# A fused attention and gated-MLP kernel on one core: where the normalization of v runs, and in which order its weights arrive

## The chip, the cores and the metric

The kernel runs on one core of a Trainium2 chip. The metric is the time of one execution on the device in microseconds (us). Five executions were timed. One execution was recorded by the hardware profiler; every duration below comes from that record. The engines are named as the profile does: PE is TensorE's matmul (PEld its loading of weights), DVE is VectorE, ACT is ScalarE, POOL is GpSimd, and SP is SyncE, which here only issues DMAs. POOL issues DMAs too, between its own computations and in the same order of instructions.

## The reference

Batch 8, 8 heads, sequence 576, head dimension 64. Linear attention with a learned feature map, then a gated MLP with a spatial (over the sequence) matrix:

```python
def phi(x):
    proj = np.einsum('bhsd,df->bhsf', x, w_phi)                  # d_feat 128
    proj = proj - np.max(np.abs(proj), axis=-1, keepdims=True)
    return np.concatenate([np.exp(proj), np.exp(-proj)], axis=-1)
q_p, k_p = (phi(q), phi(k))
kv = np.einsum('bhsf,bhsd->bhfd', k_p, v)
z = np.sum(k_p, axis=2)
num = np.einsum('bhsf,bhfd->bhsd', q_p, kv)
den = np.einsum('bhsf,bhf->bhs', q_p, z)[..., None] + 1e-06
x = num / den                                                    # heads side by side: 576 x 512
h = np.maximum(x @ w_in, 0.0)                                    # 576 x 1024
u, v = h[..., :d_ff // 2], h[..., d_ff // 2:]
v_n = (v - mean(v)) / np.sqrt(var(v) + 1e-06)                    # over the 512 columns
v_s = np.einsum('ts,bsd->btd', w_spatial, v_n) + b_spatial[None, :, None]
out = (u * v_s) @ w_out                                          # 576 x 512
```

## The kernel before

The sequence of a batch is cut into four blocks of 128 positions and a tail of 64. Work on q, k and the attention goes by units: a unit is two heads of one batch (the main blocks), four units to a batch, and one more unit holds the tails of two batches. Units are numbered in order: 0 and 1 are batch 0, 2 is the tails of batches 0 and 1, 3 and 4 batch 0 again, 5 to 8 batch 1, 9 the tails of batches 2 and 3, 10 to 13 batch 2, and so on.

step(i) (line 636) writes the instructions of one step of a software pipeline. At step i different stages of several units meet: keys (projection by TensorE, maxima mk by VectorE at line 279, features kf by ScalarE, and a_scale at line 299: em by ScalarE, then vs, v times em, by GpSimd at line 307, vst for tails at line 322), queries (maxima mq, and their split into two bf16 halves, mhl, at lines 296 and 297, which GpSimd does from unit 5 on), maxima (a transpose of mhl, line 328), query features, the products kv and num, and xT.

After each stage, fill (line 620) takes tasks of the MLP from a queue by a credit of TensorE time. b_tasks (line 592) makes the tasks of one batch: v (b_v and b_v_tail: matmul, relu by ScalarE, mean and variance by VectorE), the root 1/sqrt(var + 1e-6) on GpSimd (root, line 454: add, pow, product with the mean, change of sign), the normalization of v by one multiply-add per block (line 465, on GpSimd; vn for the four blocks, vnt for the tail), u (b_u), the spatial matmuls (b_s, lines 524 and 525: four blocks of vn and the tail) with their product by u on VectorE (line 527), and the output matmuls of the batch before. Batch 0 also transposes the spatial matrix there (transpose_spatial) and copies the spatial bias, four copies by ScalarE, into the row of w_spT that a row of ones in vnt picks up.

From batch 2 on (XB) k and q are transposed by DMAs that SP issues (cross, line 116), three steps ahead, and the query maxima are merged into the query projection through the wide weights wm. These hold, per head, w_phi and a row that subtracts the maximum; weights_with_max writes them on GpSimd at steps 6 and 7, twelve small instructions. A copy of half of q's transpose (q_even, tile qt) goes by another DMA on SP, one step ahead of the unit.

Loads are given to steps by at(step, ...), and stand after the step's other instructions: k, q and the weights on POOL's queue (with a cast from fp32 to bf16), v on SP's. What goes through pin stays in the order in which it was written on its engine; the other instructions are put in order by a scheduler. In the profile all that goes through pin has the line 61, so it is told apart by its tile.

Of the kernel before, what the change touches and what calls it, by code (L numbers as in the profile page):

```python
# [8 lines left out]
FP32 = mybir.dt.float32  # L9
# [7 lines left out]
def kernel(  # L17
# [116 lines left out]
    for n, t in enumerate((k, q)):  # L134
        for i in range(2):
            pin(nc.sync.dma_start)(out=tails[i * TL:(i + 1) * TL, n * H:(n + 1) * H, :], in_=tail_ap(t, i))
    load_v(0, 0)
# [43 lines left out]
    for i in range(2):  # L181
        fill_vnt(i, nc.gpsimd.tensor_copy)
    for x in ("k", "q"):
        pin(nc.gpsimd.tensor_copy)(out=half_tile(x, 0, 0)[:, 2:4], in_=first[x, 2])
# [9 lines left out]
    wsp = s2.tile([P, NB, T0], BF16, tag="vn", name="wsp", bufs=2)  # L194
    wspr = cpool.tile([P, NB, TL], BF16)
    wspt = s2.tile([TL, S], BF16, tag="ob", name="wspt", bufs=6)
    bsp_row = s2.tile([P, S], FP32, tag="xT", name="bsp_row", bufs=3)
    nc.sync.dma_start(out=bsp_row[TL:TL + 1, :], in_=moe_b_spatial)
    nc.sync.dma_start(out=bsp_row[0:1, :], in_=moe_b_spatial)
# [10 lines left out]
    def transpose_spatial(i):  # L210

        pt = psum.tile([P, S], BF16, tag="bank", name="pt")
        if i < NB:
            sc = POS[i]
            for tp, c in enumerate(POS):
                nc.tensor.transpose(out=pt[:, tp * P:(tp + 1) * P], in_=wsp[:, c, bass.ds(sc, P, step=NB)],
                                    identity=ident)
            nc.tensor.transpose(out=pt[:, T0:S], in_=wspt[:, bass.ds(sc, P, step=NB)],
                                identity=ident[:TL, :TL])
            nc.vector.tensor_copy(out=w_spT[:, i, :], in_=pt)  # L220
            return
        for bl in range(2):
            lo = bl * TL
            for tp, c in enumerate(POS):
                nc.tensor.transpose(out=pt[lo:lo + TL, tp * P:(tp + 1) * P], in_=wspr[:, c, :], identity=ident)
            nc.tensor.transpose(out=pt[lo:lo + TL, T0:S], in_=wspt[:, T0:S], identity=ident[:TL, :TL])
            nc.vector.tensor_copy(out=w_spT[lo:lo + TL, NB + bl, :], in_=pt[lo:lo + TL, :])
        for bl, row in ((0, TL), (1, 0)):
            r = slice(row, row + 1)
            pin(nc.scalar.copy)(  # L230
                out=w_spT[r, NB + bl, 0:T0].rearrange("o (a b p) -> o a b p", a=2, b=2),
                in_=bsp_row[r, 0:T0].rearrange("o (p b a) -> o a b p", a=2, b=2))
            pin(nc.scalar.copy)(out=w_spT[r, NB + bl, T0:S], in_=bsp_row[r, T0:S])


    def merged(u):
        return u["pair"] and u["b"] >= XB

    def weights_with_max(n):
        for j in range(4 * n, 4 * n + 4, 2):  # L240
            pin(nc.gpsimd.tensor_copy)(out=wm[:, j, :], in_=wphi2[:, 0:F])
            pin(nc.gpsimd.tensor_tensor)(out=wm[:, j + 1, :], in0=wphi2[:, F:2 * F], in1=sel[:, j + 1, :], op=ALU.add)
            pin(nc.gpsimd.tensor_copy)(out=wm[D:D + 2 * H, j, :], in_=sel[0:2 * H, j, :])
# [40 lines left out]
    def a_queries(u):  # L284

        m, early = mhl[u["i"] % NM], u["i"] < EARLY
        if not early:
            mq = small.tile([P, H], FP32, tag="mq", name="mq")
        for half in range(2):
            pq = by_token(u["qT"], half)  # L290
            if early and half == 0:
                mq = pq[:, 0, 0:H]
            nc.vector.tensor_reduce(out=mq[:, 4 * half:4 * half + 4], in_=pq, axis=AX.X, op=ALU.max,  # L293
                                    apply_absolute_value=True)
        eng = nc.vector if early else nc.gpsimd
        eng.tensor_copy(out=m[:, 0:H], in_=mq)
        eng.tensor_tensor(out=m[:, H:2 * H], in0=mq, in1=m[:, 0:H], op=ALU.subtract)

    def a_scale(u):
# [3 lines left out]
        if u["pair"]:  # L303
            pj = u["pj"]
            vs = feat.tile([P, 2, H, DA], BF16, tag="vs", name="vs", bufs=4)
            for s in range(2):
                nc.gpsimd.tensor_tensor(out=vs[:, s, :, 0:D], in0=st[u["b"]]["v"][:, pj * H:(pj + 1) * H, :],  # L307
                                        in1=em[:, s, :].unsqueeze(2).to_broadcast([P, H, D]), op=ALU.mult)
            nc.gpsimd.tensor_copy(out=vs[:, :, :, D:DA], in_=em.unsqueeze(3).to_broadcast([P, 2, H, 2]))
# [144 lines left out]
    def root(mv, r, n):  # L454

        var = small.tile([P, NB, 1], FP32, tag="var", name="var")
        rs = small.tile([P, NB, 2], FP32, tag="rs", name="rs")
        nc.gpsimd.tensor_scalar(out=var[r, 0:n], in0=mv[r, 0:n, 1:2], scalar1=1e-6, scalar2=None, op0=ALU.add)
        nc.gpsimd.tensor_tensor(out=rs[r, 0:n, 0:1], in0=var[r, 0:n], in1=neghalf[r, 0:n].unsqueeze(2), op=ALU.pow)
        nc.gpsimd.tensor_tensor(out=var[r, 0:n], in0=mv[r, 0:n, 0:1], in1=rs[r, 0:n, 0:1], op=ALU.mult)  # L460
        nc.gpsimd.tensor_scalar(out=rs[r, 0:n, 1:2], in0=var[r, 0:n], scalar1=-1.0, scalar2=None, op0=ALU.mult)
        return rs

    def normalize(dst, src, rs):
        nc.gpsimd.tensor_scalar(out=dst, in0=src, scalar1=rs[:, 0:1], scalar2=rs[:, 1:2],  # L465
                                op0=ALU.mult, op1=ALU.add)

    def b_v(b, j):
# [7 lines left out]
        v_mm(lambda kc: d["xT"][:, kc, j * P:(j + 1) * P], d["vr"][j], slice(0, P), stats, d["mv"][:, j, :])  # L476

    def b_root(b):
        st[b]["rs"] = root(st[b]["mv"], slice(0, P), NB)

    def b_ln(b, j):
        d = st[b]
        normalize(d["vn"][:, j, :], d["vr"][j], d["rs"][:, j, :])

    def b_v_tail(g, bls):
# [6 lines left out]
        rstd = root(mv, r, 1)  # L492
        for bl in bls:
            r = slice(bl * TL, (bl + 1) * TL)
            normalize(vnt[g % 2][r, bl, :], vr[r], rstd[r, 0, :])
# [96 lines left out]
    def b_tasks(b):  # L592
# [8 lines left out]
        ts.append((0.0, lambda: b_root(b)))  # L601
        if b == 0:
            ts += [(0.3, lambda i=i: transpose_spatial(i)) for i in range(NB + 1)]
        for y in range(NB):
            ts += ns[y:y + 1] + outs[2 + y:3 + y] + us[y:y + 1]
# [75 lines left out]
    at(1, load_v, 1)  # L681
    at(2, load, "k", 1, 0)
# [4 lines left out]
    at(4, load_weight, wspt, moe_w_spatial[T0:S, :])  # L687
    at(5, tail_scale, 0, 1)
    at(5, load_weight, wsp, rows[:, :, 0:T0])
    at(5, load_weight, wspr, rows[:, :, T0:S])  # L690
    at(6, load_weight, w_in_bf[:, :, 0:HALF], cols[:, :, 0:HALF])
    at(8, load_weight, w_out_bf, moe_w_out.rearrange("(kc p) f -> p kc f", p=P))
    for u in units:
        i = u["i"]
        if not u["pair"] and u["g"] > 0:
            early = 1 if u["g"] > 1 else 0
            at(i - AT - early, load_tail, "k", u["g"])
            for x in ("q", "v"):
                at(i - AT + 1 - early, load_tail, x, u["g"])
        if u["pair"] and u["b"] >= XB:  # L700
            if u["pj"] == 0:
                for n, (x, y) in enumerate((("k", 0), ("q", 0), ("k", 1), ("q", 1))):
                    at((4, 4, 6, 7)[n] if u["b"] == XB else i - AB + n, load, x, u["b"], y)
# [4 lines left out]
    at(6, weights_with_max, 0)  # L708
    at(7, weights_with_max, 1)
# [39 lines left out]
```

## Time and profile before

| | |
|---|---|
| median of 5 runs | 285.83 us (284.72 to 286.02) |
| the profiled execution | 285.86 us, of it span 283.77 us |
| mean granted clock of TensorE | 0.987 of full |
| busy: PE, DVE, ACT, POOL | 260.4, 231.4, 219.4, 200.6 us |
| vn and vnt on POOL, line 465 | 40 instructions, 0.77 us each |
| vs on POOL, line 307 | 64 instructions, 1.04 us each |
| pow of the root on POOL, line 459 | 8 of 1.05 us (128x4) and 8 of 0.58 us (64x1) |
| the other three instructions of a root on POOL | 0.19 to 0.25 us each |
| the wm writes on POOL | 12 instructions, 0.28 to 0.43 us each |
| one load issued on POOL | 0.56 to 0.82 us |
| the four bias copies on ACT | 1.11 us (two of 1x512), 0.24 us (two of 1x64) |
| DMA engines, mean busy share | 7 to 9 tenths in each slice up to 205 us |

The span is the time from the first to the last recorded instruction. Busy time is the union of an engine's instructions. Matmuls are pipelined, so PE counts as busy also where it only waits for a matmul to drain; the distance between the starts of two matmuls says more. In the chain of waits each piece is the work that the next one waited for, or its neighbour on the same engine, followed back from the end. A line of a timeline gives start, duration, engine, line of the kernel, operation, output and input tiles and their shapes, and in brackets how long the engine stood idle before it and what released it.

### The profile page before, as it was taken

The page shows a single profiled execution, that of the slowest core. Times are in us where ns is not written, and L with a number is a line of the kernel's source. Part 1 is how long each engine was busy: PE and PEld are TensorE (multiplying, and loading weights), DVE is VectorE, ACT ScalarE, POOL GpSimd, SP SyncE. Part 2 cuts the span into 40 slices and gives each one's busy share as a digit, 9 for nine tenths or more (in the row PEclk, how much of TensorE's full clock was granted, in tenths as well). Part 3 has the DMA queues.
Part 4 walks back from the last instruction along what each step waited for, and adds up shares of the span by engine and source line. Part 5 has one row for each costly group of instructions (what it writes and reads, how often), then busy time and mean ns, then how long its engine had stood idle before and what let it go on. Part 6 is the DMA issues. An engine that isn't in the chain of part 4 may idle for free.

```text
span 283.8 us, 8175 instructions
## 1 busy us (share of the span) xinstructions
PE 260.4 (92%) x3042; PEld 173.2 (61%) x3042; DVE 231.4 (82%) x576; ACT 219.4 (77%) x499; POOL 200.6 (71%) x362
## 2 busy tenths in 40 slices
PE   2768987987999999999999999999999999999993
PEld 1457875764666576666666675666666765654441
DVE  7969996875699988998889989997889897566441
ACT  5669996979299997899889987899789977723601
POOL 5897999999958895799949984889548832411710
PEclk9979999999799999999999999999999999999999
DMA  8998999999977999979989999999765301120305
GB/s 195 218 229 102 157 140 242 142 145 215 173 96 154 131 239 195 161 217 208 191 110 130 205 192 162 233 204 225 101 121 132 86 2 58 55 76 37 112 3 185
DMA packets 85148, 42.43 MB, mean 150 GB/s; under 512 B 52146, under 2 KB 80498, under 8 KB 85108
## 3 DMA queue, kind: packets, MB, share of 16 engines
q1 hardware_dynamic: 60020, 30.95, 54.0%
q0 software_dynamic: 24928, 10.89, 36.9%
q8 instruction: 24, 0.39, 0.6%
q14 instruction: 16, 0.13, 0.2%
q10 hardware_dynamic: 160, 0.07, 0.1%
HBM read 32.85 MB, written 9.44 MB: 149 GB/s over the span
## 4 chain that ended last, share of the span: by engine, by line
PE 61%; POOL 16%; ACT 7%; DVE 6%; DMA 5%; issue 3%; SPq 0%; POOLq 0%; ACTq 0%; DVEq 0%
PE ps L524 10%; PE po L549 9%; PE pv L448 9%; PE ps L267 6%; PE pu L503 6%; ACT kf L282 4%; PE pv L379 4%; PE pn L399 4%; PE pq L345 3%; POOL vs L307 3%; DMA q_bf<-in_q_dram 3%; PE ps L525 2%; POOL vst L61 2%; DVE stats L451 2%; DMA first<-in_q_dram 2%
## 5 line engine op out<-in xcount | busy, mean ns | idle before, releaser
L282 ACT ACTIVATE kf<-ps 128x512 bf16<-128x512 f32 x144 | 76.2, 634 | 9.8 <-DVE mk L279 9.4
L307 POOL TENSOR_TENSOR vs<-v_f,em 128x512 bf16<-128x512 f32 x64 | 65.4, 1043 | 19.4 <-ACT em L302 17.7
L366 ACT ACTIVATE qf<-pq 128x512 bf16<-128x512 f32 x128 | 66.6, 619 | 10.6 <-PE pq L345 8.5
L279 DVE TENSOR_REDUCE mk<-ps 128x4 f32<-128x512 f32 x72 | 47.6, 677 | 1.2 <-PE ps L267 0.5
L293 DVE TENSOR_REDUCE mq<-ps 128x4 f32<-128x512 f32 x62 | 39.8, 679 | 2.5 <-PE ps L267 2.2
L524 PE MATMUL ps<-w_spT,vn 128*128 128x512 bf16 x128 | 34.5, 386 | 2.9 <-POOL vn L465 2.7
L527 DVE TENSOR_TENSOR uT<-ps,uT 128x512 bf16<-128x512 f32 x32 | 21.9, 686 | 17.0 <-PE ps L525 17.0
L451 DVE BATCH_NORM_STATS2 stats<-vr 128x6 f32<-128x512 bf16 (+1 forms) x40 | 26.7, 683 | 7.4 <-ACT vr L450 7.1
L549 PE MATMUL po<-w_out_bf,uT 128*128 128x512 bf16 x128 | 32.4, 379 | 0.0
L503 PE MATMUL pu<-xT,w_in_bf 128*128 128x512 bf16 x128 | 32.1, 379 | 0.0
L448 PE MATMUL pv<-w_in_bf,xT 128*128 128x512 bf16 x128 | 31.5, 379 | 0.1
L450 ACT ACTIVATE vr<-pv 128x512 bf16<-128x512 f32 (+1 forms) x40 | 23.5, 615 | 7.6 <-PE pv L448 6.5
L379 PE MATMUL pv<-vs,kf 128*128 128x66 bf16 x512 | 24.3, 193 | 1.3 <-ACT kf L282 1.3
L465 POOL TENSOR_SCALAR vn<-vr,rs 128x512 bf16<-128x512 bf16 x32 | 24.3, 768 | 1.1
L390 DVE TENSOR_TENSOR x<-pn,rc 128x256 bf16<-128x256 f32 x64 | 24.8, 416 | 0.3
L399 PEld LDWEIGHTS <-qf 128*128 128x128 bf16 x512 | 20.4, 98 | 6.7 <-issue 0.8
L505 ACT ACTIVATE uT<-pu 128x512 bf16<-128x512 f32 x32 | 19.6, 639 | 4.9 <-PE pu L503 3.2
L379 PEld LDWEIGHTS <-kf 128*128 128x128 bf16 x512 | 21.8, 97 | 2.4 <-issue 1.5
L552 ACT COPY ob<-po 128x512 f32<-128x512 f32 x18 | 11.0, 612 | 14.9 <-PE po L549 8.4
L399 PE MATMUL pn<-kv,qf 128*128 128x66 bf16 x512 | 22.0, 195 | 0.3 <-ACT qf L366 0.3
L381 PE MATMUL pv<-vst,kf 128*128 128x66 bf16 x128 | 21.2, 191 | 0.0
L524 PEld LDWEIGHTS <-vn 128*128 128x128 bf16 x128 | 11.8, 98 | 14.1 <-POOL vn L465 4.8
(133 smaller groups left out, 573.4 us busy)
## 6 DMA issues: line engine op xcount, KB each, us to landing
out_dram<-ob SPq DMA_DIRECT2D x32, 256.0 KB, 2.5
v_f<-in_v_dram SPq DMA_DIRECT2D x14, 512.0 KB, 7.2
k_bf<-in_k_dram POOLq DMA_DIRECT2D x14, 256.0 KB, 6.0
q_bf<-in_q_dram POOLq DMA_DIRECT2D x14, 256.0 KB, 6.3
qt<-qT_b SPq DMA_DIRECT2D x24, 64.0 KB, 4.3
v_tl<-in_v_dram SPq DMA_DIRECT2D x8, 128.0 KB, 3.4
v_f<-in_v_dram SPq DMA_DIRECT2D x1, 1024.0 KB, 9.9
w_in_bf<-in_moe_w_in_dram POOLq DMA_DIRECT2D x2, 512.0 KB, 9.3
```

The lines of the kernel that those rows point to most:

```text
L279: nc.vector.tensor_reduce(out=u["mk"][:, hs], in_=pk, axis=AX.X, op=ALU.max, apply_absolute_value=True)
L282: nc.scalar.activation(out=u["kf"][:, s, hs, :], in_=pk, func=AF.Exp, bias=0.0, scale=sc)
L293: nc.vector.tensor_reduce(out=mq[:, 4 * half:4 * half + 4], in_=pq, axis=AX.X, op=ALU.max, apply_absolute_value=True)
L307: nc.gpsimd.tensor_tensor(out=vs[:, s, :, 0:D], in0=st[u["b"]]["v"][:, pj * H:(pj + 1) * H, :], in1=em[:, s, :].unsqueeze(2).to_broadcast( ...
L366: nc.scalar.activation(out=qf[:, s], in_=pq, func=AF.Exp, bias=0.0, scale=sc)
L379: nc.tensor.matmul(out=pv[:, hh, s, :], lhsT=u["kf"][:, s, 4 * hh + c, :], rhs=u["vs"][:, s, 4 * hh + c, :], start=(c == 0), stop=False)
L399: nc.tensor.matmul(out=pn[:, pos, :], lhsT=u["qf"][hh][:, s, pos, :], rhs=d["kv"][:, 2 * u["pj"] + hh, s, :], start=(s == 0), stop=(s == 1))
L448: nc.tensor.matmul(out=pv[r], lhsT=lhs(kc), rhs=w_in_bf[:, kc, HALF:DFF], start=(kc == 0), stop=(kc == KC - 1))
L451: nc.vector.bn_stats(out=stats[r], in_=dst[r])
L503: nc.tensor.matmul(out=pu, lhsT=w_in_bf[:, kc, dc * P:(dc + 1) * P], rhs=d["xT"][:, kc, :], start=(kc == 0), stop=(kc == KC - 1))
L524: nc.tensor.matmul(out=ps, lhsT=d["vn"][:, sp, cs], rhs=w_spT[:, sp, 0:T0], start=(sp == 0), stop=False)
L549: nc.tensor.matmul(out=po[r], lhsT=lhs(dc), rhs=w_out_bf[:, dc, :], start=(dc == 0), stop=(dc == KC - 1))
```

## The change

Five things are changed together.

1. The normalization moves from GpSimd to VectorE, as (v - mean) times 1/sqrt, so that the product with the mean and the change of sign drop out of the root. The add of 1e-6 goes to VectorE too; of the root only the pow stays on GpSimd. In the list of tasks the root of the tail and that of the blocks stand right behind the last v, and the normalizations (tail and block 0 behind the third u, blocks 1 to 3 behind the fourth) just ahead of the spatial matmuls; before they were spread between u and output tasks.
2. The wide weights wm are written by two ScalarE copies before the first unit, and one GpSimd instruction of 128x512 after step 1, in place of twelve on GpSimd at steps 6 and 7.
3. The bias rows are loaded by SP ahead of v, and the bias copies stand after steps 1 and 2 in place of batch 0's tasks.
4. The spatial matrix is loaded in one piece (128 x 4 x 576) at step 4, in place of two at step 5; the order of the loads up to step 9 changes: the first half of w_in (for u) one step sooner, the tails of batches 2 and 3 one step later, the spatial tail rows at step 6 in place of 4, k and q of batch 2 at steps 7, 7, 8 and 9 in place of 4, 4, 6 and 7, w_out at 9 in place of 8, and k and q of batch 3 one step later.
5. mhl and vs on GpSimd keep their written order (pin).

```diff
+    bsp_row = s2.tile([P, S], FP32, tag="xT", name="bsp_row", bufs=3)
+    for r in (TL, 0):
+        pin(nc.sync.dma_start)(out=bsp_row[r:r + 1, :], in_=moe_b_spatial)
     load_v(0, 0)
     load_tail("v", 0)
     load_v(0, 1)
...
+    def alternate(t, i):
+        return t.rearrange("p (j two) f -> p j two f", two=2)[:, :, i, :]
+
+    pin(nc.scalar.copy)(out=alternate(wm, 0), in_=wphi2[:, 0:F].unsqueeze(1).to_broadcast([P, NP, F]))
+    pin(nc.scalar.copy)(out=alternate(wm[D:D + 2 * H], 0), in_=alternate(sel[0:2 * H], 0))
+
+    def odd_weights():
+        pin(nc.gpsimd.tensor_tensor)(out=alternate(wm, 1), in0=alternate(sel, 1),
+                                     in1=wphi2[:, F:2 * F].unsqueeze(1).to_broadcast([P, NP, F]), op=ALU.add)
...
-    wsp = s2.tile([P, NB, T0], BF16, tag="vn", name="wsp", bufs=2)
-    wspr = cpool.tile([P, NB, TL], BF16)
+    wsp = s2.tile([P, NB, S], BF16, tag="vn", name="wsp", bufs=2)
...
-        eng.tensor_copy(out=m[:, 0:H], in_=mq)
-        eng.tensor_tensor(out=m[:, H:2 * H], in0=mq, in1=m[:, 0:H], op=ALU.subtract)
+        pin(eng.tensor_copy)(out=m[:, 0:H], in_=mq)
+        pin(eng.tensor_tensor)(out=m[:, H:2 * H], in0=mq, in1=m[:, 0:H], op=ALU.subtract)
...
-    def root(mv, r, n):
-
+    def with_eps(mv, r, n):
         var = small.tile([P, NB, 1], FP32, tag="var", name="var")
-        rs = small.tile([P, NB, 2], FP32, tag="rs", name="rs")
-        nc.gpsimd.tensor_scalar(out=var[r, 0:n], in0=mv[r, 0:n, 1:2], scalar1=1e-6, scalar2=None, op0=ALU.add)
-        nc.gpsimd.tensor_tensor(out=rs[r, 0:n, 0:1], in0=var[r, 0:n], in1=neghalf[r, 0:n].unsqueeze(2), op=ALU.pow)
-        nc.gpsimd.tensor_tensor(out=var[r, 0:n], in0=mv[r, 0:n, 0:1], in1=rs[r, 0:n, 0:1], op=ALU.mult)
-        nc.gpsimd.tensor_scalar(out=rs[r, 0:n, 1:2], in0=var[r, 0:n], scalar1=-1.0, scalar2=None, op0=ALU.mult)
+        nc.vector.tensor_scalar(out=var[r, 0:n], in0=mv[r, 0:n, 1:2], scalar1=1e-6, scalar2=None, op0=ALU.add)
+        return var
+
+    def root(var, r, n):
+        rs = small.tile([P, NB, 1], FP32, tag="rs", name="rs")
+        pin(nc.gpsimd.tensor_tensor)(out=rs[r, 0:n], in0=var[r, 0:n], in1=neghalf[r, 0:n].unsqueeze(2), op=ALU.pow)
         return rs
 
-    def normalize(dst, src, rs):
-        nc.gpsimd.tensor_scalar(out=dst, in0=src, scalar1=rs[:, 0:1], scalar2=rs[:, 1:2],
-                                op0=ALU.mult, op1=ALU.add)
+    def normalize(dst, src, mv, rs):
+        pin(nc.vector.tensor_scalar)(out=dst, in0=src, scalar1=mv[:, 0:1], scalar2=rs, op0=ALU.subtract, op1=ALU.mult)
...
-        ts.append((0.0, lambda: b_root(b)))
+        ts.append((0.0, lambda: b_root_tail(g, [bl])))
         if b == 0:
             ts += [(0.3, lambda i=i: transpose_spatial(i)) for i in range(NB + 1)]
-        for y in range(NB):
-            ts += ns[y:y + 1] + outs[2 + y:3 + y] + us[y:y + 1]
+        ns.insert(0, (0.0, lambda: b_ln_tail(g, [bl])))
+        ts += [(0.0, lambda: b_root(b))] + outs[2:3] + us[:1] + outs[3:4] + us[1:2] + outs[4:]
+        ts += us[2:3] + ns[:2] + us[3:] + ns[2:]
...
     at(1, load_v, 1)
+    at(1, odd_weights)
+    at(1, spatial_bias, 0)
+    at(2, spatial_bias, 1)
...
-    at(4, load_weight, wspt, moe_w_spatial[T0:S, :])
+    at(4, load_weight, wsp, rows)
     at(5, tail_scale, 0, 1)
-    at(5, load_weight, wsp, rows[:, :, 0:T0])
-    at(5, load_weight, wspr, rows[:, :, T0:S])
-    at(6, load_weight, w_in_bf[:, :, 0:HALF], cols[:, :, 0:HALF])
-    at(8, load_weight, w_out_bf, moe_w_out.rearrange("(kc p) f -> p kc f", p=P))
+    at(5, load_weight, w_in_bf[:, :, 0:HALF], cols[:, :, 0:HALF])
+    at(5, load_tail, "k", 1)
+    at(6, load_tail, "v", 1)
+    at(6, load_tail, "q", 1)
+    at(6, load_weight, wspt, moe_w_spatial[T0:S, :])
+    at(7, load, "k", 2, 0)
+    at(7, load, "q", 2, 0)
+    at(8, load, "k", 2, 1)
+    at(8, load_v, 2, 0)
+    at(9, load, "q", 2, 1)
+    at(9, load_v, 2, 1)
+    at(9, load_weight, w_out_bf, moe_w_out.rearrange("(kc p) f -> p kc f", p=P))
...
-                    at((4, 4, 6, 7)[n] if u["b"] == XB else i - AB + n, load, x, u["b"], y)
+                    at(i - AB + n + (u["b"] == 3), load, x, u["b"], y)
...
-    at(6, weights_with_max, 0)
-    at(7, weights_with_max, 1)
```

spatial_bias(bl) holds two of the four bias copies that stood at the end of transpose_spatial, for one row each.

## The prediction

> **What bounds the kernel now.** I read four views: the page's busy shares, the chain of waits over the first quarter, the timeline of the matmuls where that chain passes, and busy time by windows. TensorE is busy 92% of the span, but not evenly. I compared the start-to-start times of its matmuls with their own unblocked pace (0.86 us for four 128x512, 0.44 us for four 128x256): of some 35 us lost between first and last matmul, about 24 lie before 80 us, 10 between 80 and 265, 1 after that. So the start is what can be shortened, and the chain of waits says by whom (start us, us, what; "x" counts instructions):
>
> ```profile
> 29.89 0.56 POOL wspt L61
> 30.46 1.39 POOL k_tl L61 x2
> 31.85 0.76 POOL k_bf L61
> 32.61 0.74 POOL q_bf L61
> 33.36 2.07 POOL vs L307 x2
> ...
> 43.58 0.20 POOL mhl L297
> ...
> 65.50 1.06 POOL rs L459
> 66.63 0.22 POOL var L460
> 66.93 0.27 POOL rs L461
> 67.29 0.77 POOL vn L465
> 68.06 0.82 POOL q_bf L61
> 68.93 2.27 POOL vn L465 x3
> 71.25 0.39 PE ps L524
> ```
>
> From 29.89 to 71.25 us the chain stays on GpSimd without a hole: loads that it issues, vs, the wm writes, root, vn. TensorE waits for it twice, here at the first spatial matmuls (timeline of TensorE; in brackets the idle time before):
>
> ```profile
> 43.83 0.23 PE L328 MATMUL pt<-ident,mhl 128*128 128x128 bf16 x1 [1.56 <-POOL mhl L297]
> ...
> 59.46 0.38 PE L267 MATMUL ps<-wphi,kT_b 128*128 128x256 bf16 x2 [1.15 <-ACT qf L366]
> ...
> 69.75 0.39 PE L524 MATMUL ps<-w_spT,vn 128*128 128x512 bf16 x1 [1.25 <-POOL vn L465]
> ...
> 71.48 0.39 PE L525 MATMUL ps<-w_spT,vnt 128*128 128x512 bf16 x1
> ```
>
> The windows view then shows a stretch at half clock (0.50, the third number from the right), directly behind that idle time:
>
> ```profile
> 72.00:75.00 3.00, 3.00 (x34) 2.02 (x32) 2.70 (x9) 0.00 (x0) 2.92 (x7) 0.50 1.47 211
> ```
>
> Later TensorE runs at its pace, and VectorE, which gets the new work, is nearly as full: over seven 20 us windows from 80 to 220 it is busy 128.7 of 140 us, so it has 11.3 us idle, 2.4 per batch of 29.9 us (starts of the first L524 of batches 1 to 5: 105.75, 135.70, 164.78, 195.42, 225.25).
>
> **What each part is worth.** Base: the profiled execution took 285.86 us, 283.77 of it span; the median of the five runs is 285.83, so sums against the one hold for the other.
>
> First spatial matmuls. Four unblocked L524 from 67.81 (end of the four L267 that start at 67.37) would let L525 start at 68.67; it starts at 71.48. Gain 2.81. In the changed program's order vn 1 to 3 stand on VectorE behind the keys' maxima, which end here at 67.5; with all that is gained before, both sides move alike. The root is in time: GpSimd loses between 29.9 and 66.6 one load issue (wspr 0.73), twelve wm writes (45.38 to 47.56 and 51.06 to 53.16: 4.28), variance, product, sign and vnt of the tail (1.6) and the variance of the batch (0.3), 6.9 in all, and three load issues (0.8 each) go behind the root; em of the tail unit (54.2), both vst (4.6), mhl and the two pow (1.63) then end near 61. I take 2.81; bounds 0 and 2.81.
>
> The clock. Half rate lasted 3.41 us; with the idle time gone that is 1.7 us more. Bounds 0 and 1.7; I take 1.7, for the first such stretch (17.1 to 20.5) also stands behind TensorE idling.
>
> L328 at 43.83. Ahead of mhl the change takes wspt (0.56), two loads of batch 2 (1.52), wspr (0.73) and q_tl (1.41) off GpSimd and puts one w_in load (0.83) there: 3.4 us. But vs at 33.36 can't start before its em, at 31.68, so only 1.7 to 2.2 of that arrive: mhl near 41.6 where TensorE comes at 42.1. The wait was 1.72; I take 1.3 because ScalarE is later (below). Bounds 0 and 1.72.
>
> L267 at 59.46 waits for a bank that ScalarE frees late, and ScalarE stood from 55.91 to 58.44 in the four bias copies, which move. Gain up to 1.31. Against it: the k load of batch 2 moves from 31.79 to about 46.8 on GpSimd (after load of wspt, vs and mhl of step 7); landing 6 us later, transposes from 53, which land in 2.4 to 5.4: 56 to 59 where TensorE wants the keys near 56.5. I take 0.8; bounds -1.3 (as late again) and 1.31.
>
> The end. L524 from 268.73 would reach L525 at 269.59; it starts at 270.70. Gain 1.11: VectorE has nothing else there, one variance add (0.17 by the aggregate rows), GpSimd's pow (1.05), then five normalizations end near 268.
>
> Costs at the start. Two bias copies (1.11 and 0.24, means of their rows) move to 20.5 us, between qf and kf on a ScalarE that is then packed to 34 with 0.51 and 0.41 idle: 0.35 late (0 to 1.35), with kf and em queued behind. The other two fit the 1.15 idle at 14.1, and the two wm copies the 1.78 before 7.57. The odd wm write is a GpSimd operation over 512 elements (vs, 1.04) ahead of vst and the loads of batch 1: the q load, waited for at 25.3, comes 1 us later; 0.3 (0 to 1.1), since VectorE, packed from 20 to 42, was not yet asking for it. On SyncE two bias rows (1.16 and 0.23) pass ahead of v; v queues behind tails in any case, and I count nothing; uncovered it is part of that 1.1.
>
> The later q load. The second half of batch 2's q moves on GpSimd from 48.05 behind the root, near 60.5. It lands 6.2 to 12.7 us later by its kind's rows; I take 67. SyncE is in order, and behind the transpose that waits for it stand the v load and the copy qt of unit 10 (62.80 now). That copy then goes at 68.5 and lands 4.3 later at 72.8, where VectorE, 6 us early, asks for it at 71.2 (77.14 now), and the maxima queue behind. Cost 1.5 (0 to 4).
>
> VectorE in batches 1 to 6. Five normalizations and two small adds per batch. No row shows a two-scalar normalization on VectorE. Nearest is a single-source bf16 copy within SBUF (columns: min/median/max ns):
>
> ```profile
> L332 DVE COPY qt<-qT_b x24: 283/284/1576, 78.2 to 240.8; 16x512 bf16<-16x512 bf16 x24
> ```
>
> Its mean is 0.405; the high bound is L451's full read of 512 elements, 0.69. By 0.405 a batch gets 5 x 0.405 + 2 x 0.17 = 2.4 us, just the 2.4 idle. In batches 1, 3 and 5 it falls ahead of an L527 wait (up to 1.2 us idle) and behind work that TensorE doesn't ask for at once: nothing, at most 0.7 each. In batches 2 and 4 the changed order has vnt, vn 0, two key maxima, then vn 1 to 3, while TensorE runs vn 0, four L267, then vn 1. In batch 2 now the second maximum ends at 136.60; plus 0.7 for the two in front and 0.4 for itself vn 1 is ready at 137.7, where TensorE comes at 136.4: 1.3 us, twice. Less 0.4 for L332 copies that collide less with GpSimd (0.12 x 24 is 2.9 at most): cost 2.2. A new wait, vnt for rs, should cost nothing: in batch 2 rs ends at 130.4 now and vnt would stand near 134.2; were it late, the key maxima queue behind it. Low bound -1.5; high: 5 x (5 x 0.69 + 0.34) less 11.3 idle, 7.6.
>
> Rows of the same copy between 0.283 and 1.576 show that something blocks it. The Trainium skill ("SBUF — State Buffer", section "SBUF: two separate sides") says that VectorE in a two-port mode and GpSimd exclude each other for a whole instruction on a shared port pair, which speaks against moving the work while vs stays on GpSimd. If both groups of each of five batches met a vs (1.04) at its start, VectorE would lose 10 us and the sum would be near 290; by the copy's mean it is the one below.
>
> Sum: -2.81 - 1.7 - 1.3 - 0.8 - 1.11 = -7.7; +0.35 + 0.3 + 1.5 + 2.2 = +4.35; 285.86 - 3.35 = **282.5 us**.
>
> **Rivals.** (A) The added work is free: the late copy is covered and VectorE takes it all in idle time. For: 11.3 us idle, much of it directly behind the place (L527 waits 17.0 us in all). Against: the order in batches 2 and 4. 285.86 - 2.81 - 1.7 - 1.72 - 1.31 - 1.11 + 0.65 = 277.9.
>
> (B) VectorE becomes the bound between 80 and 225: slower. At 0.69 a normalization a batch gets 3.8 for 2.4 idle, 1.4 x 5 = 7.0, plus the 2.6 in batches 2 and 4, less nothing. 285.86 - 7.7 + 2.15 + 9.6 = 289.9. It begins at 0.41 each, where the idle time is used up, and turns the sign when VectorE's whole cost passes 7.7 - 2.15 = 5.55, at 0.53 each. For: windows up to 97% full already (80 to 100). Against: median 0.284.
>
> (C) The loads give the start back: keys late at 59 and the copy qt 5 us late, so that only the end and some of the clock are left: the later load costs 4.5 where I have 1.5, 285.5, no change.
>
> **Numbers.** Forecast 0.50, its own range 280.2 (halfway to A) to 284.8; A 0.17; B 0.20; C 0.13. A measurement of this kernel can tell 0.3%, 0.86 us, from no change. Faster: forecast, A and a little of C, 0.67; the same: most of C, 0.12; slower: B and the rest, 0.21. The range reaches to A's side at 278.0 and into B to 287.5; beyond are about 0.2.
>
> **What would show it.** Right: no L328 wait near 43; no wait of L524 (L540 now) for vn in batch 0 and at the end; no half clock after 21 us; GpSimd near 155 us busy (200.6 less 30.4 of normalization, 10.9 of root, 4 of wm and 0.7, plus 1.0) and VectorE near 250 (231.4 + 16 + 2.7). Normalizations of 0.28 to 0.45. TensorE waits for VectorE's vn in batches 2 and 4, and VectorE for qt near 70. Wrong: normalizations over 0.5, or windows from 80 to 220 with VectorE at 99% and TensorE under its pace; or the half clock still there.

## The result, and the profile after

The changed kernel takes 287.13 us (median of 28 executions, 285.05 to 289.05), the kernel before 284.75 (median of 54, 281.81 to 287.15). The ratio is 1.0093, 95% interval 1.0073 to 1.0114: slower by 0.9%. The forecast was 282.5 and faster. Medians here and below are over all executions of a kernel; the ratios leave out those that took over 1.5% longer than its fastest, among them three of the six of norm_only and two of together_q (522 and 904 us).

The one profiled execution of each shows none of this: 285.38 us after (span 283.6), 285.86 before. The profiled execution of before was one of its longer ones, that of after one of its shortest. So the two traces are good for where time comes and goes, and not for the sum. The page of after, its busy shares and the chain of waits by engine:

```profile
PE 260.6 (92%) x3042; PEld 173.2 (61%) x3042; DVE 249.0 (88%) x632; ACT 220.8 (78%) x501; POOL 155.7 (55%) x262
...
PE 51%; DVE 22%; ACT 9%; DMA 8%; issue 3%; SPq 2%; POOL 2%; DVEq 0%; ACTq 0%; POOLq 0%
```

GpSimd, 16% of the chain before, is down to 2%; VectorE, 6% before, now has 22%. The chain did not get shorter, it changed engine. The timeline of TensorE over the first quarter of after (the matmuls that stood in the prediction's fences; L328, L524 and L525 are now L334, L540 and L541):

```profile
42.35 0.23 PE L334 MATMUL pt<-ident,mhl 128*128 128x128 bf16 x1
...
65.94 0.38 PE L540 MATMUL ps<-w_spT,vn 128*128 128x512 bf16 x1
67.09 1.04 PE L540 MATMUL ps<-w_spT,vn 128*128 128x512 bf16 x3 [0.77 <-DVE vn L61]
67.96 0.38 PE L541 MATMUL ps<-w_spT,vnt 128*128 128x512 bf16 x1
```

The wait for mhl is gone (1.56 before), the first vnt matmul starts at 67.96 instead of 71.48. A wait for vn is still there, now for VectorE. The windows view (the granted clock is the third number from the right):

```profile
18.00:22.00 4.00, 4.00 (x39) 3.44 (x38) 2.33 (x6) 3.97 (x8) 4.00 (x6) 0.50 0.58 139
...
72.00:75.00 3.00, 3.00 (x27) 1.77 (x25) 2.56 (x7) 2.28 (x6) 0.00 (x0) 1.00 1.46 95
```

The half clock at 72 to 75 us is gone; the one near the start is there, and longer than in the profile of before (6.83 us in all, 3.41 before). Last, 95 to 235 us as one window, before and then after (columns: TensorE, its weight loads, VectorE, ScalarE, GpSimd):

```profile
95.00:235.00 140.00, 138.34 (x1692) 92.90 (x1691) 127.60 (x307) 123.76 (x290) 105.71 (x194) 1.00 1.03 162
```

```profile
95.00:235.00 140.00, 135.58 (x1645) 90.32 (x1641) 132.45 (x328) 120.17 (x282) 78.87 (x137) 1.00 0.97 158
```

TensorE does less there in the same time, 1645 matmuls against 1692, while VectorE goes from 91% to 95%.

The sharpest measure came from the starts of matmuls: of the first spatial matmul of each batch (b0 to b7; the first L524 or L540) and the last matmul of all. In us, computed from the timelines:

| kernel, profile | b0 at | b0 to b1 | b1 to b7 | b7 to last | last at |
|---|---|---|---|---|---|
| before | 68.11 | 37.64 | 162.98 | 10.11 | 278.84 |
| before, second profile | 66.56 | 37.37 | 162.98 | 10.10 | 277.01 |
| after | 65.94 | 35.93 | 167.82 | 9.00 | 278.69 |
| after, second profile | 66.03 | 37.50 | 167.86 | 9.00 | 280.39 |

From b1 to b7 the same kernel repeats within 0.04 us. The change loses 4.8 to 4.9 us there, in both its profiles; it gains 1.1 at the end. What varies is the time up to b1.

### The profile page after: what moved, and what is told of

Its sections match the earlier page's. It is cut to its first block, busy times and chain, and to the rows that moved or that the text cites. A ratio compares the mean times of both kernels' runs of the same rounds, so it can differ in the third digit from the quotient of the medians.

```text
span 283.6 us, 8091 instructions
## 1 busy us (share of the span) xinstructions
PE 260.6 (92%) x3042; PEld 173.2 (61%) x3042; DVE 249.0 (88%) x632; ACT 220.8 (78%) x501; POOL 155.7 (55%) x262
## 4 chain that ended last, share of the span: by engine, by line
PE 51%; DVE 22%; ACT 9%; DMA 8%; issue 3%; SPq 2%; POOL 2%; DVEq 0%; ACTq 0%; POOLq 0%
PE ps L540 9%; PE pv L454 7%; PE po L565 7%; PE pu L519 5%; ACT kf L288 5%; DVE mk L285 5%; PE ps L273 5%; PE pv L385 3%; DVE vn L61 3%; DMA q_bf<-in_q_dram 3%; PE pn L405 2%; DVE mq L299 2%; PE pq L351 2%; PE ps L541 2%; ACT qf L372 2%
## 5 line engine op out<-in xcount | busy, mean ns | idle before, releaser
L540 PE MATMUL ps<-w_spT,vn 128*128 128x512 bf16 x128 | 34.5, 380 | 2.9 <-DVE vn L61 2.9
L61 POOL TENSOR_TENSOR rs<-var,neghalf 64x1 f32<-64x1 f32 (+1 forms) x16 | 12.6, 792 | 30.0 <-DVE var L462 23.0
L385 PE MATMUL pv<-vs,kf 128*128 128x66 bf16 x512 | 25.2, 195 | 1.4 <-ACT kf L288 1.2
L385 PEld LDWEIGHTS <-kf 128*128 128x128 bf16 x512 | 22.5, 98 | 3.0 <-issue 1.8
L540 PEld LDWEIGHTS <-vn 128*128 128x128 bf16 x128 | 11.5, 97 | 14.6 <-DVE vn L61 6.9
```

The source lines that it names most:

```text
L61: return lambda *a, **kw: tc.keep_in_program_order(start(*a, **kw))
L385: nc.tensor.matmul(out=pv[:, hh, s, :], lhsT=u["kf"][:, s, 4 * hh + c, :], rhs=u["vs"][:, s, 4 * hh + c, :], start=(c == 0), stop=False)
L540: nc.tensor.matmul(out=ps, lhsT=d["vn"][:, sp, cs], rhs=w_spT[:, sp, 0:T0], start=(sp == 0), stop=False)
```

## The experiments

Theory 1: the normalization on VectorE in batches 1 to 6 costs more than the start and the end gain. It has two forms: (a) by its place, a normalization being held when it starts beside a vs of GpSimd, or standing ahead of something that TensorE asks for; (b) by capacity, VectorE being full. Rival 2: the moved loads and copies, or the pins, cost the time. Rival 3: what is gained at the start is lost whatever VectorE does.

**Each half of the change alone, and the normalization only at both ends.**

norm_only is the kernel before with part 1. rest_only is the changed kernel with root, normalization and task order of before. norm_ends chooses by batch:

```diff
+    def on_vector(b):
+        return b in (0, B - 1)
...
-        normalize(d["vn"][:, j, :], d["vr"][j], d["mv"][:, j, :], d["rs"][:, j, :])
+        if not on_vector(b):
+            normalize_pool(d["vn"][:, j, :], d["vr"][j], d["rs"][:, j, :])
+            return
+        normalize(d["vn"][:, j, :], d["vr"][j], d["mv"][:, j, :], d["rs"][:, j, :])
```

> The kernel before with part 1 alone: normalization and the add of 1e-6 on VectorE, tasks in the changed order, loads, wide weights, bias copies and pins as before. Theory 1 (the normalization on VectorE in batches 1 to 6 takes what the start gains: its 0.52 us each as profiled, and TensorE waits behind it): slower than before by 1 to 5 us, since the first spatial matmuls (2.8 at most) and the end (1.1) gain here too, but the GpSimd work ahead of them stays. Rival 2 (the moved loads and copies or the pins cost it): same as before or up to 3 us faster.

> The changed kernel with part 1 undone: root and normalization on GpSimd in the order of before, parts 2 to 5 kept. Theory 1: faster than before by 1.5 to 4 us (L328 wait and the twelve wm writes gone from GpSimd's chain, so the first spatial matmuls come sooner), no gain at the end, windows from 80 to 220 us as before (VectorE near 146 of 160 us from 80 to 240). Rival 2: slower than before, 286 or more, with the same loss between 85 and 230 us as in the changed kernel.

> The changed kernel with the normalization on VectorE for batches 0 and 7 alone; batches 1 to 6 have root and normalization on GpSimd in the order of before. Theory 1: the gain at the start (some 5 us at 80 us) and at the end (1.1) both stay and nothing is given back: 278 to 281 us, 0.98 to 0.99 of the time before. Rival 2: 284 to 288, the loss between 85 and 230 us is still there. Rival 3 (what is gained at the start is lost whatever VectorE does, because VectorE or the DMA engines set the pace from 80 us on): 283 to 285.

| kernel | median | ratio to before, interval | b0 at | b0 to b1 | b1 to b7 |
|---|---|---|---|---|---|
| norm_only | 290.62 (289.49 of the three that count in the ratio) | 1.0153 (1.0094 to 1.0212) | 70.30 | 35.48 | 169.87 |
| rest_only | 285.00 | 1.0009 (0.9984 to 1.0034) | 63.94 | 39.09 | 163.59 |
| norm_ends | 282.40 | 0.9946 (0.9912 to 0.9980) | 66.42 | 37.94 | 163.60 |

Theory 1 holds against rival 2: with the normalization on GpSimd in batches 1 to 6, b1 to b7 is 163.6, 0.6 above before; with it on VectorE 167.8 or more (norm_only's 169.87 contains a half-clock stretch from 168.1 to 171.5 us). norm_only is slower, as theory 1 expected. But rest_only gained nothing where 1.5 to 4 us were expected, and norm_ends stayed above its 278 to 281. (norm_only comes to b0 late: it keeps the wait at mhl, 1.43 us, with half clock from 45.2 to 48.7 us behind it in this profile.) rest_only reaches b0 earlier than both profiles of before, norm_ends no later than the earlier one, and both take longer from there to b1. VectorE in norm_ends:

```profile
72.57 0.41 DVE L420 COPY xT<-pt 128x512 bf16<-128x512 bf16 x1
75.63 0.41 DVE L337 COPY qT_b<-pt 16x512 bf16<-16x512 bf16 x1 [2.64 <-DMA qt<-qT_b]
```

It stands for 2.64 us until the copy qt of unit 10 lands, which needs the q that the change loads later. In rest_only it stood 5.04.

**Second profiles.** after_again and before_again are the two kernels unchanged.

> The changed kernel once more, for a second profile: 285 to 289 us. The two profiles on hand are of the same length, while the medians differ by 2.4 us; if the changed kernel's loss from 80 to 230 us is a matter of VectorE, this profile loses there as much as the first one or more (5 to 9 us) and keeps the gain at 80 us; if the start varies, the gain at 80 us is smaller here.

> The kernel before once more, for a second profile. 282 to 286 us. If the half-clock stretch at 71.7 us and the waits at 43.8 and 59.5 us of the first profile belong to the program, they are here again; if not, the terms that the forecast took from them (1.7, 1.3 and 0.8) were too large.

after_again took 287.10, its loss from b1 to b7 is that of the first profile, and VectorE waited 1.95 for the same qt where the first profile had 0.38. before_again took 283.96. It has the wait at mhl (1.70 lost), that of L267 (1.28) and the half clock behind the first spatial matmuls again; they belong to the program. It does not have the one near the start.

**Which batches.** on_vector(b) is changed to `b % 2 == 0 or b == B - 1` in norm_even and `b == 0 or b % 2 == 1` in norm_odd.

> The changed kernel with the normalization on VectorE in batches 0, 2, 4, 6 and 7, on GpSimd (order of before) in 1, 3 and 5. Both profiles of the changed kernel lose about 0.5 us at the normalizations of batches 2 and 4 each, where no vs of GpSimd runs beside them. Theory 1a (place: what is lost is lost where a normalization starts beside a vs and is held until that ends): 282.4 of the kernel with batches 0 and 7 alone plus about 1, so 282.5 to 284. Theory 1b (capacity: every batch's 2.9 us of added VectorE work costs alike): plus half of the 4.5, so 284 to 285.5.

> The same with VectorE in batches 0, 1, 3, 5 and 7, GpSimd in 2, 4 and 6. In the changed kernel one normalization of batch 3 takes 2.23 us and two of batch 5 1.13 each, all beside vs, and the start of the following matmuls falls back by 2.4 and 1.2 us there. Theory 1a: 282.4 plus 3 to 4, so 285 to 287, clearly slower than the kernel with the even batches. Theory 1b: the same as that with the even batches, 284 to 285.5.

norm_even: 283.07, ratio 0.9953 (0.9913 to 0.9993), b1 to b7 164.54. norm_odd: 286.70, ratio 1.0104 (1.0056 to 1.0151), b1 to b7 167.11. Over the 163.60 of norm_ends the even batches cost 0.94 and the odd ones 3.51, though each batch adds the same work on VectorE: it matters more where the work stands than how much it is. The starts of the first spatial matmuls say between which batches (us; b1 to b2 and b6 to b7 agree within 0.02 in these five):

| kernel | b2 to b3 | b3 to b4 | b4 to b5 | b5 to b6 |
|---|---|---|---|---|
| norm_ends | 29.08 | 31.08 | 30.00 | 26.11 |
| norm_even | 29.58 | 31.16 | 30.33 | 26.15 |
| norm_odd | 30.19 | 31.60 | 30.90 | 27.10 |
| after | 30.61 | 31.61 | 31.18 | 27.10 |
| together (below) | 31.05 | 29.96 | 31.00 | 26.14 |

One thing these runs don't separate: with the engine of the normalization the order of a batch's tasks changes too (part 1 of the change), so "on VectorE" means both here. The timeline of all engines in batch 3 of after shows one place:

```profile
160.98 0.41 PE L433 MATMUL pn<-kv,qf_t 128*64 128x66 bf16 x8 [0.35 <-DVE mq L299]
...
161.44 2.89 DVE L61 TENSOR_SCALAR vn<-vr,mv,rs 128x512 bf16<-128x512 bf16 x3
161.47 2.05 POOL L61 TENSOR_TENSOR vs<-v_f,em 128x512 bf16<-128x512 f32 x2
162.43 0.38 PE L540 MATMUL ps<-w_spT,vn 128*128 128x512 bf16 x1
...
163.73 1.05 PE L540 MATMUL ps<-w_spT,vn 128*128 128x512 bf16 x3 [0.92 <-DVE vn L61]
```

The first of the three normalizations lasts 2.23 us: it starts just before the two vs and ends only with them, at 163.7. The next two take 0.33 each. TensorE, which needed vn 1, stands 0.92. Places like this lie behind b3 and b5, where norm_odd loses 0.52 and 0.99. The other 2.01 of its 3.51 are lost ahead of b3 and b5, before the held normalizations: TensorE waits there for the maxima mq ahead of b3 (0.27 and 0.41 us in norm_odd; the first line above is the second of them in after, 0.35) and for kf of ScalarE ahead of b5 (0.43 and 0.55, against one wait of 0.43 in norm_ends). All instances (columns: min/median/max ns):

```profile
L61 DVE TENSOR_SCALAR vn<-vr,mv,rs x32: 393/406/2230, 63.9 to 269.0; 128x512 bf16<-128x512 bf16 x32
```

The median is 0.406, the mean 0.530. In after all over 0.42 stand beside a vs: one of 2.23 in batch 3, two of 1.13 in batch 5, one of 1.12 in batch 0, and of the tails (vnt) 0.88 in batch 0 and 0.49 in batch 4. The second profile has the same ones.

**The late q load.** ends_q is norm_ends with that load one step sooner, where GpSimd has a hole (it issues it at 50.28 instead of 60.37); after_q and rest_q do the same to the changed kernel and to rest_only.

```diff
     at(8, load, "k", 2, 1)
+    at(8, load, "q", 2, 1)
     at(8, load_v, 2, 0)
-    at(9, load, "q", 2, 1)
```

> The kernel with VectorE's normalization in batches 0 and 7 alone, and the second q load of batch 2 given to step 8 in place of 9, so that GpSimd issues it at about 51.7 us, in a hole, and not behind the two pow at 60.4. Theory (the late q load keeps VectorE waiting for the copy qt of unit 10 up to 75.6 us, and TensorE loses 1.1 there and some behind it): that wait is gone, 280 to 281.3 us, 1 to 2.5 us less than with the load at step 9. Rival (the wait is hidden by the later pace): the same as with the load at step 9, 282 to 283.

> The changed kernel with the second q load of batch 2 at step 8 in place of 9 and nothing else. The late load as a separate loss: 284 to 285.2 us, ratio to before 0.998 to 1.002, 2.3 to 2.8 us less than the changed kernel, as it gave with VectorE's normalization in batches 0 and 7 (2.8) and with five together (2.4). Rival (VectorE's later work hides it): 286 to 287.

> The changed kernel with part 1 undone (normalization on GpSimd everywhere, order of before) and the second q load of batch 2 at step 8. With the load at step 9 this kernel was as fast as before (1.0009), its trace 5 us ahead of that of before between 45 and 75 us and 2.7 ahead from 95 on. If the late load is what took it: 281 to 283 us, ratio 0.985 to 0.994. If the normalization on VectorE in batch 0 is needed for the start to count: 284 to 285, ratio 0.996 to 1.002.

| with the load at step 9 | at step 8 |
|---|---|
| norm_ends 282.40, 0.9946 | ends_q 279.63, 0.9851 (0.9807 to 0.9896) |
| rest_only 285.00, 1.0009 | rest_q 281.07, 0.9916 (0.9880 to 0.9953) |
| changed kernel 287.13, 1.0093 | after_q 284.99, 1.0044 (1.0014 to 1.0075) |

VectorE in ends_q goes on without a wait:

```profile
71.34 0.41 DVE L420 COPY xT<-pt 128x512 bf16<-128x512 bf16 x1
71.67 0.40 DVE L337 COPY qT_b<-pt 16x512 bf16<-16x512 bf16 x1
```

The load costs 2.7 us in norm_ends and 2.6 in rest_only (by the ratios), which is where the gain of parts 2 to 5 went. In the changed kernel it is 1.4 by the ratios, 2.1 by the medians, a little under the 2.3 to 2.8 expected. The step of the load is not all that decides the wait: in the profile of ends_q_tog (below; 283.93 us, its median is 280.69) VectorE stands 2.53 us before the same copy qT_b, though the load is early (the profile names a matmul as what ended that wait). By its median ends_q is the fastest of the kernels tried; ends_q_tog and ends_q_ob, below, can't be told from it by their ratios.

**Out of the way of vs.** together puts the five normalizations of a batch in one place; together_q has the early q load too, ends_q_tog does it in ends_q.

```diff
-        ts += us[2:3] + ns[:2] + us[3:] + ns[2:]
+        ts += us[2:3] + ns + us[3:]
```

> The changed kernel with all five normalizations of a batch behind the third u, where it has two there and three behind the fourth. Same VectorE work, same loads. In batches 3 and 5 of the changed kernel the second group meets vs (161.44 and 224.43 us) and the first does not; joined to the first it should be done before vs starts, and in batches 2 and 4 no maxima stand between vn 0 and vn 1. Theory 1a (place beside vs): most of the 4.2 us that the normalization costs in batches 1 to 6 comes back: 283 to 285 us, ratio to before 0.995 to 1.0. Theory 1b (capacity of VectorE): 286.5 to 288 as the changed kernel, ratio 1.007 to 1.011.

> The same with the second q load of batch 2 at step 8. Theory 1a with the late load as a separate loss of 2.8: 280 to 282.5, and the sum of both effects should be additive. Theory 1b: 283.5 to 285.

> VectorE's normalization in batches 0 and 7 alone, all five together behind the third u, and the q load at step 8. In batch 0 the tail and block 0 are still held by vs (0.88 and 1.12 us) but blocks 1 to 3 follow at once, so TensorE's wait of 0.94 between vn 0 and vn 1 should go; the keys' maxima come 1 us later. 278.7 to 279.8 us if it goes, 279.6 or more if the maxima are what is late next.

together: 285.88, 1.0040 (1.0011 to 1.0070), b1 to b7 165.48. In batches 1 to 7 a vs no longer holds any normalization by more than 0.1 us (two of 0.64 and 0.65 stand beside loads that GpSimd issues), and 2.4 of the 4.2 us come back, from b3 to b4 and b5 to b6. The time is between what the two forms expected. together_q: 283.49, 0.9959 (0.9930 to 0.9989), so the two effects add up (no profile of it is read). ends_q_tog: 0.9831 (0.9786 to 0.9876), median 280.69: no difference from ends_q that can be told. Where a part of the other 1.9 us of together arises shows ahead of its b3, all engines:

```profile
162.37 1.61 DVE L61 TENSOR_SCALAR vn<-vr,mv,rs 128x512 bf16<-128x512 bf16 x4 [0.19 <-POOL rs L61]
...
163.64 0.42 PE L433 MATMUL pn<-kv,qf_t 128*64 128x66 bf16 x8 [0.56 <-ACT kf L288]
163.91 1.27 DVE L299 TENSOR_REDUCE mq<-ps 128x4 f32<-128x512 f32 x2
163.92 2.05 POOL L61 TENSOR_TENSOR vs<-v_f,em 128x512 bf16<-128x512 f32 x2
164.63 0.29 PE L385 MATMUL pv<-vs,kf 128*128 128x66 bf16 x4 [0.57 <-DVE mq L299]
```

The normalizations end just as vs starts, as meant. But the maxima mq stand behind them on VectorE, and TensorE waits twice, 0.56 and 0.57. The second wait names mq. The first is put down to kf of ScalarE, which is busy until 163.59; the first mq starts only at 163.91, after that wait has ended, so it can't be mq's. Why ScalarE is late there no run isolates.

**Less work on VectorE.** The copies ob of batches 0 to 6 all go to ScalarE, in together_q and, as a control, in ends_q.

```diff
-        (nc.vector.tensor_copy if turn[0] else nc.scalar.copy)(out=ob[r], in_=po[r])
+        (nc.vector.tensor_copy if turn[0] and b == B - 1 else nc.scalar.copy)(out=ob[r], in_=po[r])
```

> The kernel with five normalizations together and the early q load, with all copies ob of batches 0 to 6 on ScalarE in place of every second on VectorE: some 1.5 us less VectorE work in a batch. With the five together no normalization of batches 1 to 6 is held by vs, and TensorE still falls back by some 2.3 us there, behind late maxima. If VectorE's queue is what is left: 280.5 to 282.3 us, 1 to 2.5 less than with the copies shared (283.49). If it is something else, or ScalarE becomes late in its turn: 283.3 or more.

> The same copies on ScalarE in the kernel with VectorE's normalization in batches 0 and 7 alone and the early q load (279.63). There VectorE has as much work as before in the other batches, and the trace loses only 0.6 us between 95 and 235. If VectorE's queue matters only with the added work: no gain, 279.3 to 280.5, or a loss if ScalarE becomes late. If VectorE is late anyhow: 278 to 279.

together_q_ob: 282.45, 0.9957 (0.9924 to 0.9990), against 283.49 and 0.9959 of together_q: 1 us by medians, nothing by ratios, and a median between the two outcomes that were expected. ends_q_ob: 279.92, 0.9870 (0.9826 to 0.9914): nothing. The traces say more. VectorE is busy 180.95 of the 200 us from 40 to 240 in together_q_ob, 186.77 in together, and yet b1 to b7 takes 165.12 against 165.48. Taking 5.8 us of work away returns 0.4. (The q load is early in the one and late in the other; from b1 to b7 that made no difference over 0.04 in two pairs, 167.82 and 167.86, 163.60 and 163.59.) This speaks against VectorE's total as the rest of the loss. It does not rule out ScalarE, which got the copies: in together_q_ob it is busy without a break before kf in batch 3, and TensorE waits 0.36 and 0.56 for kf there, though in ends_q the same copies cost only 0.2 (163.79 against 163.59). That the rest lies in what stands ahead of the maxima in VectorE's queue is likely for the waits that name mq, and open for those that name kf.

**Another form of the instruction.** two_source leaves everything and writes the normalization with two tensor inputs:

```diff
-        pin(nc.vector.tensor_scalar)(out=dst, in0=src, scalar1=mv[:, 0:1], scalar2=rs, op0=ALU.subtract, op1=ALU.mult)
+        pin(nc.vector.scalar_tensor_tensor)(out=dst, in0=src, scalar=mv[:, 0:1], in1=rs.to_broadcast([dst.shape[0], HALF]),
+                                            op0=ALU.subtract, op1=ALU.mult)
```

> The changed kernel with the normalization as an instruction with two tensor inputs (v and 1/sqrt, broadcast along the row, with the mean as a per-row scalar), the same values. In the trace of the changed kernel only single-source instructions within SBUF are held by vs; bn_stats, and all that reads PSUM or two tensors, keep their time beside vs. If the hold belongs to the form: every normalization 0.65 to 0.72 us, none over 0.8 beside vs, and a longer kernel, 287 to 291, since the 30 in batches 1 to 6 cost 8 us more and save 3.3 of holding. If any normalization within SBUF is held: some of 1.1 to 2.3 us again.

Its one execution took 295.54 us. The form of the instruction does not free it: the second of the two outcomes came. The timeline of batch 1, GpSimd and VectorE:

```profile
104.07 2.48 POOL L61 TENSOR_TENSOR vs<-v_f,em 128x512 bf16<-128x512 f32 x2 [1.58 <-ACT em L308]
104.31 3.46 DVE L61 SCALAR_TENSOR_TENSOR vn<-vr,mv,rs 128x512 bf16<-128x512 bf16 x3
106.51 0.67 POOL L61 CAST vs<-em 128x32 bf16<-128x32 f32 x1
107.12 0.70 POOL L61 CAST mhl<-mq 128x8 bf16<-128x8 f32 x1
```

Free of GpSimd it takes 0.73 to 0.75; beside vs 1.35 and 1.53 here, up to 2.36 elsewhere. This form is held as well, and it holds GpSimd in turn: the casts of 0.2 us take 0.7. The Trainium skill, "GPSIMD Engine Reference", section "8. Key points", names both cases, VectorE in a two-port mode or with two inputs in SBUF; these rows agree.

## Why the prediction was wrong

Three sums can be set against each other, the forecast's and the runs' (ratios times 284.75; by the medians themselves the three terms are -5.1, +5.4 and +2.1):

| | forecast | measured | from |
|---|---|---|---|
| start and end, without the q load | -7.7 + 0.65 = -7.05 | -4.2 | ends_q, 0.9851 |
| normalization in batches 1 to 6, with its order of tasks | +2.2 | +5.5 | after_q less ends_q, 1.0044 - 0.9851 |
| the later q load | +1.5 | +1.4 | changed kernel less after_q, 1.0093 - 1.0044 |
| sum | -3.35 | +2.65 | the changed kernel, 1.0093 |

The three measured rows add up by the way they are taken. What speaks for them from elsewhere: the starts of the matmuls give the normalization 4.3 from b1 to b7 (after_q against ends_q), and 1.5 from b0 to b1, this from one pair of profiles at a place where two profiles of the changed kernel differ by 1.6; the late load cost 2.7 and 2.6 in the two other pairs.

**The step that failed: VectorE in batches 1 to 6.** The text priced a normalization right in the ordinary case (0.405; the median is 0.406) and found 2.4 us of work for 2.4 us of idle time a batch. It then said of batches 1, 3 and 5 that the work falls ahead of an L527 wait and behind work that TensorE doesn't ask for at once, "nothing, at most 0.7 each", and laid its cost on batches 2 and 4, 1.3 each. It was the other way round: from b1 to b7 the even batches cost 0.94 together and the odd ones 3.51, and batch 1, which lies ahead of b1, perhaps another 1.5 (b0 to b1 is 36.67 in after_q and 35.18 in ends_q, one profile each). In batches 2 and 4 TensorE did wait for vn, 0.48 and 0.46 us. The idle time was an average over 140 us, and the place for the work was taken to be ahead of the waits for L525, 17.0 us in all in the profile of before. The waits view of after:

```profile
PEld L540 <- DVE vn L61: 6.9, 17, 1.2
...
DVE uT L543 <- PE ps L541: 5.2, 10, 1.6
```

VectorE's wait shrank to 5.2 us, so the work did go into idle time. But it stands in the queue ahead of that wait, in front of maxima that TensorE needs before, and beside vs. The hold was in the text, as a sentence on the exclusive port pair of the Trainium skill ("SBUF — State Buffer", section "SBUF: two separate sides"), with a price of 10 us if both groups of five batches met a vs. Two groups of the changed kernel's batches 1 to 6 do, for 3.3 us of VectorE's time (1.82 + 2 x 0.72 over 0.406). These rows agree with the rule, a row for it (1.576 for a copy of 0.284) was in the profile of before, and it should have been priced by the order in the queue, group by group, instead of by the copy's mean.

**The rivals.** (B) had the sign and only part of the mechanism. Its turning point, 0.53 a normalization, is just the mean that was measured (0.530), by chance: at 95% VectorE's total is not what bounds it, as far as together_q_ob can say. (A) took as free what cost 5.5. (C) was right that the q load comes late: VectorE stood 0.38 (after), 1.95 (after_again), 2.64 (norm_ends) and 3.46 us (norm_odd) for it, and 5.04 in rest_only. As the term of the sum (1.5) it was well sized; the 4.5 of (C) was not reached in the changed kernel.

**Start and end.** This term was mis-sized too, 7.05 for 4.2. The end gave 1.1 as forecast. L328 gave 1.4 (1.3 forecast) and L267 0.6 (0.8), by the starts of the same matmuls in the profiles of before and ends_q. From 60 to 75 us, with first spatial matmuls and half clock, 3.1 came instead of 2.81 + 1.7 = 4.51: vnt and vn 0 of batch 0 stand beside a vs (0.88 and 1.12 us), and vn 1 is late again. With the normalization left on GpSimd (rest_q) the same stretch gave 4.1, and b1 came at 99.58 against 100.37 in ends_q; so in these profiles VectorE gains nothing at the start. Its gain at the end is 0.8 (b7 to last 9.00, and 9.80 in rest_q). Then 0.6 of the lead is lost between b1 and b7 even with the normalization on GpSimd. And the sum was made against an execution of 285.86 that the five runs shown put at the median; over 54 runs the median is 284.75, so 1.1 of the gain had been no gain. The costs on ScalarE and of the odd wm write (0.65) can't be told from the spread at the start.

**What would show it.** Right: no mhl wait, no half clock from 71 to 75 ("no half clock after 21 us" was not quite met: the stretch near the start ran from 15.5 to 22.3), GpSimd at 155.7 and VectorE at 249.0 (155 and 250 forecast), no wait at the end, waits for vn in batches 2 and 4 and for qt near 70. Wrong: no wait for vn in batch 0, and normalizations of 0.28 to 0.45; the sign named for "wrong" was there, "normalizations over 0.5".

## What to carry to other kernels

Idle time of an in-order engine is worth something only where it stands in the queue: list, for each place where work is added, what is queued behind it and when that is asked for, and don't divide a total by the batches. Where VectorE works within SBUF, look up what GpSimd runs at that moment, for it may have to wait for all of it. When two profiles disagree with the medians, compare distances between the same matmuls in the steady part, which here repeat to 0.04 us, and when a change loses, undo it stage by stage: here the moved loads and copies with an early q load brought more than half of what was gained (rest_q, 0.9916), and the normalization on VectorE gained 0.8 us at the end, nothing at the start, and lost between. The intervals of rest_q and ends_q (0.9851) overlap.

## What the runs showed of the hardware

- The stretch at half clock near the start lasted 0, 3.41 or 6.83 us (in 4, 7 and 6 of 17 profiles; that of together_q is left out), also where the program is the same up to there: 6.83 in both profiles of the changed kernel, 0 in after_q; 3.41 and 0 in those of before, whose b0 differ by 1.55 us. No run ties it to anything in the kernel.
- Of VectorE's instructions only some that work within SBUF were held by a product of GpSimd: by vs the normalization (0.41 to 2.23) and the copy qt (0.28 to 1.58 in before), by vst, the product of the tails, one add on 128x4 (0.17 to 1.01). Beside loads that GpSimd issues they took longer too: a copy qt 0.62 (after, at 79.12), a normalization 0.65 (together, at 134.18). bn_stats, which reads SBUF and writes six numbers a row, took 0.695 at most in 20 instances beside vs (the two profiles of the changed kernel), and the reductions and products out of PSUM kept their 0.68 too.
- A held normalization came in either behind the one vs that it met (0.88, 1.12, 1.13 us), or only behind the second of two, though by the record it had started 0.02 to 0.03 us before the first (161.44 and 161.47 in after; 2.23 to 2.28 us in each of the four profiles with this place). What decides it was not tried.
- Three normalizations in a row start 0.32 us apart, though each lasts 0.40: 1.04 us for the three at 66.64.
